# Gate and up projections in a seven-product block form on pairs of segments, and the down projection in groups of two tiles

## The chip, the cores and the metric

One core of a Trainium2 chip runs the whole program in one launch. The metric is the device time of one execution in microseconds (us). A core has five engines that work side by side, each with its own queue, served in order: TensorE (PE, matrix products; its weight loads are shown as PEld), VectorE (DVE), ScalarE (ACT), GpSimd (POOL) and SyncE (SP, here the issuer of DMAs). SBUF is the on-chip memory, PSUM the memory that PE writes its products to, in banks of 128 x 512 fp32 values.

## The reference

```python
h = _layernorm(x) * (1 + ca) + sa
x = x + ga * _A_ref(h, ...)            # attention with a memory, 32 heads, 4 segments of 512 rows
h = _layernorm(x) * (1 + cb) + sb
g = jnp.einsum("bsd,df->bsf", h, w_gate)
u = jnp.einsum("bsd,df->bsf", h, w_up)
x = x + gb * jnp.einsum("bsf,fd->bsd", g * u, w_down)
```

The input is 2048 rows of 512 features, in fp32. sa, ca, ga, sb, cb and gb are six vectors made from a condition vector. The change is in the last three lines, the gated feed-forward part: w_gate and w_up are 512 x 1376, w_down is 1376 x 512.

## The kernel before

The first 522 us of the program hold the modulation vectors, the first LayerNorm, the attention and its output projection (`wo_row`, `wo_add`: the sum of attention and input, 128 rows at a time, goes to a DRAM buffer `x1d` by a DMA on L496). The last stage, from 522 us on, is the feed-forward part, and the change is there. It works on four segments of 512 rows one after the other.

Every fp32 product is made of three products of a faster type, fp32r: each operand is split into a high part (a rounded copy) and a low part (the operand less the high part), and high x high, low x high and high x low are summed in PSUM. The transposed activations of a segment are `chH` and `chL` (512 features as 4 blocks of 128, by 512 rows). 1376 features make 11 tiles (`ft`, `NF`): ten of 128 and the last of 96.

`gate_up(i)` (L1110) makes 12 matmuls for the gate and 12 for the up projection of tile i (4 blocks x 3 products, L1122), each into a bank of its own. ACT copies the gate bank to SBUF (`gs`, L1126), DVE multiplies it by the up bank (L1127), ACT makes the high part `mH` (L1130) and DVE the low part `mL` (L1131). The down projection of tile i (L1143) then takes 12 matmuls: 4 row blocks x 3 products, into four banks `acc` that stay open over all 11 tiles of the segment. `gate_up(i + 1)` is issued before the down products of tile i, so that PE has work while the other engines make `mH` and `mL`. At a segment's end DVE adds the four banks to the rows of `x1d`, loaded again (`xc`, L1155 and L1156), and the result is stored (L1157).

Weights are prepared once and then stay in SBUF. `prep(i)` (L394) loads tile i of w_gate, w_up and w_down (L400, L402), makes the high parts on DVE (L429) and the low parts on POOL (L430); w_down is first multiplied by gb (`gbb`, DVE, L435), then split on ACT (L437) and POOL (L438). Tiles 0 and 1 are prepared before the last stage, on POOL alone; tiles 2 to 10 during segment 0. `lnC(s)` (L504) is the second LayerNorm of a segment. It loads four row blocks of `x1d` and calls `ln` (L171): statistics on DVE (L178), a few small operations, the normalisation on DVE (L198), 16 transposes on PE (L88), scale and shift on ACT (`chf`, L211), then the high and low parts (for segment 0 on ACT and POOL, L218 and L219; else on DVE, L215 and L216). For segments 1 to 3 it runs inside the segment before, at tiles 3 and 6.

PSUM has eight banks. They are named by tags: `ms0`, `ms1`, `tb`, `sm`, `lq0`, `lq1`, and `lk`, which is one tile of two banks. The order in which each engine issues its instructions is set by a scheduler when the program is built; `pe()` and `pin()` (L72, L79) add an ordering after the PE instruction issued before, without a wait.

Of the kernel before, what the change touches and what calls it, by code (L numbers as in the profile page):

```python
# [17 lines left out]
P = 128  # L18
# [39 lines left out]
def tile_kernel(ctx, tc, x, wq, wk_, wv, wo, beta, w_gate, w_up, w_down, c, w_mod, out):  # L58
# [28 lines left out]
    def TP(*a):  # L87
        return pe(nc.tensor.transpose(*a))  # L88
# [4 lines left out]
    wpool = ctx.enter_context(tc.tile_pool(name="wp", bufs=1))  # L93
# [298 lines left out]
    wt = {}  # L392

    def prep(i, pool, rpool, tag, nb):  # L394

        f0, n = ft[i]
        r, raws = {}, {}
        for w, nm in ((w_gate, "g"), (w_up, "u")):
            raws[nm] = raw = rpool.tile([P, KT, P], F32, tag=tag, name=f"cr{nm}{i}", bufs=nb)
            pin(nc.sync.dma_start(raw[:, :, 0:n], w.rearrange("(k p) f -> p k f", p=P)[:, :, f0:f0 + n]))  # L400
        rawd = rpool.tile([P, D], F32, tag=tag, name=f"crd{i}", bufs=nb)
        pin(nc.sync.dma_start(rawd[0:n], w_down[f0:f0 + n, :]))  # L402
        yield 0.0
        if i < 2:
            gp = nc.gpsimd
            for nm in "gu":
                hi = pool.tile([P, KT, P], F32R, name=f"{nm}H{i}", bufs=1)
                r[nm] = (hi, pool.tile([P, KT, P], F32R, name=f"{nm}L{i}", bufs=1))
                pin(gp.tensor_copy(hi, raws[nm]))
                yield 0.0  # L410
            for nm in "gu":
                pin(gp.tensor_sub(r[nm][1], raws[nm], r[nm][0].bitcast(F32)))
                yield 0.0
            hi = pool.tile([P, D], F32R, name=f"dH{i}", bufs=1)
            lo = pool.tile([P, D], F32R, name=f"dL{i}", bufs=1)
            pin(gp.tensor_mul(rawd, rawd, gbb))
            yield 0.0
            pin(gp.tensor_copy(hi, rawd))
            yield 0.0
            pin(gp.tensor_sub(lo, rawd, hi.bitcast(F32)))  # L420
            r["d"] = (hi, lo)
            wt[i] = r
            yield 0.0
            return
        for nm in "gu":
            raw = raws[nm]
            hi = pool.tile([P, KT, P], F32R, name=f"{nm}H{i}", bufs=1)
            lo = pool.tile([P, KT, P], F32R, name=f"{nm}L{i}", bufs=1)
            pin(vec.tensor_copy(hi[:, :, 0:n], raw[:, :, 0:n]))  # L429
            nc.gpsimd.tensor_sub(lo[:, :, 0:n], raw[:, :, 0:n], hi[:, :, 0:n].bitcast(F32))  # L430
            r[nm] = (hi, lo)
            yield 0.0
        hi = pool.tile([P, D], F32R, name=f"dH{i}", bufs=1)
        lo = pool.tile([P, D], F32R, name=f"dL{i}", bufs=1)
        pin(vec.tensor_mul(rawd[0:n], rawd[0:n], gbb[0:n]))  # L435
        yield 0.0
        act.activation(hi[0:n], rawd[0:n], AF.Copy)  # L437
        nc.gpsimd.tensor_sub(lo[0:n], rawd[0:n], hi[0:n].bitcast(F32))  # L438
        r["d"] = (hi, lo)
        wt[i] = r  # L440
        yield 0.0

    def wo_load(s, pool):
        rw = []
# [59 lines left out]
    def lnC(s, pool, hpool, xpool, tag, nb):  # L504
        xt = []
        for t in range(4):
            a = xpool.tile([P, D], F32, tag=tag, name=f"x1_{s}_{t}", bufs=nb)
            nc.sync.dma_start(a, x1d[s][t])
            xt.append(a)
        yield 0.1  # L510
        return (yield from ln(pool, hpool, xt, s, cb_c, sb_c, "c", ("h{}", 1, 1), s > 0))


    pwpool, pw = open_pool(name="pw", bufs=1, reuse_waits="tile")
# [426 lines left out]
    def fill_b():  # L941
        open_b()
        pb, bc = B["pb"], B["bc"]
        while osegs[0] <= 2:
            yield None
        us2 = []
        op2 = wo_op(2, B["o", 2], us2)
        xr1 = xr_load(1, pb)
        lg = lnC(0, pb, bc, pb, "x1", 4)
        pr = prep(0, bc, pb, "cr", 3)  # L950
        mm = weave(wo_mm(1, B["us1"], xr1), lg, (3, 6, 8, 10, 12, 14))
        yield from weave(weave(mm, op2, (0, 5, 9, 13)), pr, (6, 11, 11, 13, 14, 15, 16, 18))
        yield from op2
        xr2 = xr_load(2, pb)
        B["orl_free"] = True
        yield from pr
        pr = prep(1, bc, pb, "cr", 3)
        next(pr)
        yield from weave(weave(wo_mm(2, us2, xr2), lg, (0, 2, 4, 6, 8, 10, 12, 14)), pr, (0, 2, 3, 7, 9, 16, 18))
        yield from pr  # L960
        B["nxt"] = yield from lg

    vfree, osegs = [1], [0]
    fa, fb = fill_a(), fill_b()
# [128 lines left out]
    close(B["pbpool"])  # L1093
    close(pwpool)
    close(apool)
    vec.eng = nc.vector


    pcpool, pc = open_pool(name="pc", bufs=2, reuse_waits="tile")
    PC = 12  # L1100
    btag[:] = ["ms", "tb", "ms", "sm"]
    bc = B["bc"]
    nxt = B["nxt"]
    for s in range(NSEG):
        hH, hL = nxt
        ac = psp.tile([P, 2, 512], F32, tag="lk", name=f"acc{s}", bufs=1)
        acc = [pst((P, 512), f"lq{t}", f"acc{s}{t}") for t in range(2)] + [ac[:, t] for t in range(2)]
        mids = {}

        def gate_up(i):  # L1110
            f0, n = ft[i]
            if s == 0 and 1 < i + 1 < NF:
                last_pe[0] = None
                run(prep(i + 1, pc, pc, "pt", PC))
            pss = []
            for nm in "gu":
                ps = bank(f"{nm}ps{s}_{i}")
                hi, lo = wt[i][nm]
                j = 0
                for k in range(KT):  # L1120
                    for a, b in ((hi, hH), (lo, hH), (hi, hL)):
                        nc.tensor.matmul(ps[0:n], a[:, k, 0:n], b[k], start=j == 0, stop=j == 11)  # L1122
                        j += 1
                pss.append(ps)
            gs = pc.tile([P, L], F32, tag="tsb", name=f"gs{s}_{i}", bufs=2)
            act.activation(gs[0:n], pss[0][0:n], AF.Copy)  # L1126
            vec.tensor_mul(gs[0:n], gs[0:n], pss[1][0:n])  # L1127
            mH = pc.tile([P, L], F32R, tag="pt", name=f"mH{s}_{i}", bufs=PC)
            mL = pc.tile([P, L], F32R, tag="pt", name=f"mL{s}_{i}", bufs=PC)
            act.activation(mH[0:n], gs[0:n], AF.Copy)  # L1130
            vec.tensor_sub(mL[0:n], gs[0:n], mH[0:n].bitcast(F32))  # L1131
            mids[i] = mH, mL

        gate_up(0)
        for i in range(NF):
            if i + 1 < NF:
                gate_up(i + 1)
            n = ft[i][1]
            mH, mL = mids.pop(i)
            dH, dL = wt[i]["d"]  # L1140
            for t in range(4):
                for j, (a, b) in enumerate(((mH, dH), (mL, dH), (mH, dL))):
                    nc.tensor.matmul(acc[t], a[0:n, t * P:(t + 1) * P], b[0:n, :],  # L1143
                                     start=i == 0 and j == 0, stop=i == NF - 1 and j == 2)
            if i == 3 and s + 1 < NSEG:
                last_pe[0] = None
                lg = lnC(s + 1, pc, pc if s % 2 == 0 else bc, pc, "pt", PC)
                for _ in range(10):
                    next(lg)
            if i == 6 and s + 1 < NSEG:  # L1150
                last_pe[0] = None
                nxt = run(lg)
        for t in range(4):
            xr = pc.tile([P, D], F32, tag="pt", name=f"xc{s}_{t}", bufs=PC)
            nc.sync.dma_start(xr, x1d[s][t])  # L1155
            vec.tensor_add(xr, xr, acc[t])  # L1156
            nc.sync.dma_start(out[rows(s, t), :], xr)  # L1157
    close(pcpool)
    close(B["bcpool"])

# [25 lines left out]
```

## Time and profile before

| | |
|---|---|
| three runs | 898.5, 898.92, 900.3 us; median 898.92 |
| the profiled execution, first to last instruction (span) | 898.4 us |
| last stage, first matmul to end of the last | 522.0 to 893.9 us |
| loads of a weight tile, issue to landing (median) | 2.9 to 3.6 us |

The busy time of an engine is given in us and as a share of the span, with the number of instructions. A row of a group gives line, engine and operation, the tiles written and read, their shapes, the count, busy time and mean duration in ns, then the idle time of the engine just before and what ended it. The chain that ended last is followed back from the last instruction, at each step to what released it. A row of windows gives the start and end of a stretch, its length, then the busy time of PE, PEld, DVE, ACT and POOL in it, with counts, then the granted clock of PE as a share of full speed, the busy share of the DMA engines, and GB/s. A row of the timeline gives start, duration and the instruction, with the wait before it and its releaser in brackets.

### The profile page before, as it was taken

Reading aid. Unit: us, or ns where it says so; the run is one execution under the profiler, and the core shown is the slowest. Engines: PE = TensorE matmul, PEld = TensorE weight load, DVE = VectorE, ACT = ScalarE, POOL = GpSimd, SP = SyncE. Lnnn points to the kernel's source line nnn. Section 1 sums busy time; section 2 is a strip of 40 time slices with the busy share of each in tenths; the row PEclk is TensorE's granted clock in tenths of the full one; section 3 lists DMA queues with packets and bytes.
Section 4 is the critical chain, followed back from the end, with each engine's and each line's share of the span. In section 5 each row is a group of like instructions: output and inputs, shape, how many; then the busy total and the mean of one; then the engine's idle time right before and its main releaser. Section 6 shows DMA issues by size and latency. Waiting matters only on the chain.

```text
span 898.4 us, 14218 instructions
## 1 busy us (share of the span) xinstructions
PE 870.9 (97%) x5084; PEld 620.5 (69%) x5084; DVE 523.4 (58%) x1579; ACT 406.1 (45%) x601; POOL 321.2 (36%) x470
## 2 busy tenths in 40 slices
PE   8989999989999999999999999999999999999997
PEld 5755656556665556666666678887888788878886
DVE  7698777888788877778887244552133213321112
ACT  3747757687676865777454512231112111211111
POOL 4445536466455763756337516630000000000000
PEclk8999999999999999999999999999999999999999
DMA  7654434454545555365584344321001100110011
GB/s 219 163 159 130 122 109 124 152 154 130 146 111 156 141 154 129 107 202 166 187 243 140 109 144 126 106 73 71 24 1 47 72 24 1 47 45 3 1 47 47
DMA packets 74951, 97.23 MB, mean 108 GB/s; under 512 B 10528, under 2 KB 47392, under 8 KB 74880
## 3 DMA queue, kind: packets, MB, share of 16 engines
q1 hardware_dynamic: 74736, 96.31, 36.3%
q8 instruction: 40, 0.66, 0.3%
q14 instruction: 31, 0.25, 0.1%
q10 hardware_dynamic: 144, 0.02, 0.0%
HBM read 67.98 MB, written 28.05 MB: 107 GB/s over the span
## 4 chain that ended last, share of the span: by engine, by line
PE 81%; DVE 10%; ACT 5%; issue 1%; DMA 1%; POOL 1%; SPq 0%; DVEq 0%; POOLq 0%
PE gps L1122 14%; PE acc L1143 14%; PE ups L1122 14%; PE tb L85 8%; PE q L85 6%; PE k L85 6%; DVE q L39 5%; PE wops L85 5%; PE vps L85 4%; PE kps L85 4%; PE qps L85 2%; ACT pt L331 2%; PE up L85 1%; PE mz L85 1%; PE tr L88 1%
## 5 line engine op out<-in xcount | busy, mean ns | idle before, releaser
L39 DVE CUSTOM_DVE_ANT_0 q<-q,cmask 128x384 f32<-128x384 f32 (+3 forms) x512 | 246.6, 508 | 49.3 <-PE q L85 39.2
L331 ACT ACTIVATE pt<-k 128x1024 f32<-128x1024 f32 x160 | 163.8, 1024 | 64.4 <-PE k L85 63.3
L337 POOL TENSOR_SCALAR_AFFINE_SELECT pt<-pt 128x256 f32<-128x256 f32 (+1 forms) x224 | 96.7, 446 | 166.0 <-ACT pt L331 163.6
L1127 DVE TENSOR_TENSOR gs<-gs,ups 128x512 f32<-128x512 f32 (+1 forms) x44 | 30.2, 687 | 194.9 <-PE ups L1122 194.9
L85 PE MATMUL q<-kst,qst 96*128 96x384 bf16 (+3 forms) x512 | 101.6, 299 | 11.0 <-DVE nm L39 9.7
L85 PE MATMUL k<-qst,kst 98*128 98x384 bf16 (+3 forms) x512 | 97.1, 302 | 5.0 <-ACT pt L331 4.9
L1126 ACT ACTIVATE gs<-gps 128x512 f32<-128x512 f32 (+1 forms) x44 | 26.2, 597 | 146.3 <-PE gps L1122 146.3
L1130 ACT ACTIVATE mH<-gs 128x512 fp32r<-128x512 f32 (+1 forms) x44 | 27.8, 632 | 130.4 <-DVE gs L1127 128.1
L85 PE MATMUL tb<-pt,v 128*32 128x512 f32 (+3 forms) x1024 | 75.5, 436 | 0.0
L39 DVE DVE_READ_ACCUMULATOR2_ANT nm<- 128x1 f32 x512 | 72.2, 141 | 0.0
L85 PEld LDWEIGHTS <-kst 98*128 98x128 bf16 x512 | 37.7, 98 | 49.5 <-issue 43.2
L1122 PE MATMUL gps<-chH,gL 128*128 128x512 f32 (+1 forms) x176 | 69.3, 394 | 0.0
L1122 PE MATMUL gps<-chH,gH 128*128 128x512 f32 (+1 forms) x176 | 69.3, 394 | 0.0
L1143 PE MATMUL acc<-dH,mL 128*128 128x512 f32 (+1 forms) x176 | 69.3, 394 | 0.0
L1122 PE MATMUL ups<-chH,uH 128*128 128x512 f32 (+1 forms) x176 | 69.3, 394 | 0.0
L1122 PE MATMUL gps<-chL,gH 128*128 128x512 f32 (+1 forms) x176 | 69.3, 393 | 0.0
L1143 PE MATMUL acc<-dL,mH 128*128 128x512 f32 (+1 forms) x176 | 69.2, 393 | 0.0
L1122 PE MATMUL ups<-chL,uH 128*128 128x512 f32 (+1 forms) x176 | 69.2, 393 | 0.0
L1122 PE MATMUL ups<-chH,uL 128*128 128x512 f32 (+1 forms) x176 | 69.2, 393 | 0.0
L85 PEld LDWEIGHTS <-qst 96*128 96x128 bf16 x512 | 43.1, 97 | 37.5 <-issue 13.4
L1143 PE MATMUL acc<-dH,mH 128*128 128x512 f32 (+1 forms) x176 | 65.0, 395 | 0.0
L85 PEld LDWEIGHTS tb<-pt,v 128*32 128x32 f32 x1024 | 28.7, 109 | 38.6 <-issue 33.8
(218 smaller groups left out, 1654.5 us busy)
## 6 DMA issues: line engine op xcount, KB each, us to landing
wm<-in_w_mod_dram SPq DMA_DIRECT2D x24, 256.0 KB, 4.0
kd<-k SPq DMA_DIRECT2D x16, 384.0 KB, 2.5
kst<-kd SPq DMA_DIRECT2D x32, 192.0 KB, 3.2
qd<-q SPq DMA_DIRECT2D x16, 384.0 KB, 2.9
qst<-qd SPq DMA_DIRECT2D x32, 192.0 KB, 3.6
x<-in_x_dram SPq DMA_DIRECT2D x16, 256.0 KB, 4.5
kst<-kd SPq DMA_DIRECT2D x32, 128.0 KB, 3.1
qst<-qd SPq DMA_DIRECT2D x32, 128.0 KB, 3.6
```

The lines of the kernel that those rows point to most:

```text
L39: i = getattr(self.eng, name)(*a, **k)
L85: return pe(nc.tensor.matmul(*a, **k))
L88: return pe(nc.tensor.transpose(*a))
L331: ex = act.activation(pt, kp, AF.Exp, scale=0.25)
L337: sels[u, i] = nc.gpsimd.affine_select(w, w, pattern=[[0, w.shape[1]], [1, P]], compare_op=ALU.is_ge, fill=0.0, base=0, channel_multiplier=-1)
L1122: nc.tensor.matmul(ps[0:n], a[:, k, 0:n], b[k], start=j == 0, stop=j == 11)
L1126: act.activation(gs[0:n], pss[0][0:n], AF.Copy)
L1127: vec.tensor_mul(gs[0:n], gs[0:n], pss[1][0:n])
L1130: act.activation(mH[0:n], gs[0:n], AF.Copy)
L1143: nc.tensor.matmul(acc[t], a[0:n, t * P:(t + 1) * P], b[0:n, :], start=i == 0 and j == 0, stop=i == NF - 1 and j == 2)
```

## The change

Gate and up are no longer made segment by segment. The segments form two pairs, p = 0 (segments 0 and 1) and p = 1 (2 and 3). Two tiles of one weight matrix by 512 features are seen as 2 x 2 blocks (two tiles, two halves of the features), and the transposed activations of a pair of segments as 2 x 2 blocks (two halves of the features, two segments). The product of these blocks takes seven products of blocks instead of eight, with sums of blocks on both sides. A `unit` is the gate or up projection of two tiles for a pair of segments: seven products of 6 matmuls (2 blocks of 128 features x 3 products). Its products are called by number: Z (2), Y (5, then 3), X (1, 6, 7, 4). ACT copies of open banks and DVE sums of them give the four blocks of the result.

- `build(p)` makes the seven right-hand pieces of a pair from the fp32 activations `hfs`: eight differences on POOL, high parts on ACT, low parts on DVE. For p = 0, pieces 1 and 2 come from `lnC(0)`.
- `wprep(n)` prepares the seven left-hand pieces of a unit: one load of 512 KB, four additions or subtractions of 256 elements per partition on POOL, then high parts on ACT and low parts on POOL of 512, 256 and 1024 elements. Three slots (`wh0` to `wh2`, `wl0` to `wl2`) hold them; unit n uses slot -n mod 3. `prepare(n + 2)` is issued along unit n.
- Units 0 to 7 are tiles (2,3), (4,5), (6,7), (8,9) of pair 0, gate and up in turn. Unit 8 (`x_unit`) is tile 10 of pair 1 in plain products (`direct`, 48 matmuls), prepared by `xprep`. Units 9 to 18 are tiles (0,1) to (8,9) of pair 1.
- Pair 0 begins with tiles 0, 1 and 10 in plain products: `direct` for segment 0, 24 matmuls each, then the transposes of segment 1's LayerNorm, down chunks of segment 0, then `direct` for segment 1. The second half of `direct` uses product 1 of the first half (`q0_*`) and pieces 5 and 3.
- The product of gate and up is made on POOL where both lie in SBUF (three of four blocks of a pair of units) and on DVE for the one still in PSUM. `split` makes `mH` on ACT and `mL` on DVE.
- `down` takes two tiles at a time (one for tile 10): a chunk of 6 matmuls for a row block goes to one of four banks in turn (`lq0`, first half of `lk`, `lq1`, second half of `lk`), and DVE adds it to an accumulator in SBUF (`xa`), which was loaded from `x1d`. After tiles (8,9) the row block is stored, and for p = 0 the accumulator is loaded for p = 1. `d()` issues one chunk from a list, at the points of a unit given in `DS`.
- `wdprep` loads and splits w_down tile by tile for each pair, so twice: product and low part on DVE, high part on ACT. The down weights of tiles 0, 1 and 10 of pair 0 lie in slot `wh1`/`wl1`.
- `lnC` keeps fp32 activations; segment 1's small operations go to DVE. It runs in the start for segment 1 and in units 1 to 6 for segments 2 and 3.

The diff, cut to its core:

```diff
+    units = [(0, nm, i) for i in range(2, LAST, 2) for nm in "gu"]
+    CH = len(units)
+    units += [(1, "x", LAST)] + [(1, nm, i) for i in range(0, LAST, 2) for nm in "gu"]
...
+    def wprep(n, tag, pool, rpool):
...
+        pin(nc.sync.dma_start(raw.rearrange("p k r c -> p k (r c)"), views["gu".index(nm)][:, :, 0:2 * P]))
...
+        gp.tensor_add(S[:, 0], A(1, 0), A(1, 1))
+        gp.tensor_sub(S[:, 1], S[:, 0], A(0, 0))
+        gp.tensor_sub(S[:, 2], A(0, 0), A(1, 0))
+        gp.tensor_sub(S[:, 3], A(0, 1), S[:, 1])
+        top = raw[:, :, 0].rearrange("p (c k) f -> p c k f", c=2)
+        for d, v in ((slice(4, 6), top), (6, A(1, 1)), (slice(0, 4), S)):
+            act.activation(wh[:, d], v, AF.Copy)
+            gp.tensor_sub(wl[:, d], v, wh[:, d].bitcast(F32))
...
+    def six(ps, wh, wl, wi, n, bh, bl, first, last):
+        c = 0
+        for k in range(2):
+            w, l = (a[(slice(None), *wi(k), slice(0, n))] for a in (wh, wl))
+            for a, b in ((w, bh), (l, bh), (w, bl)):
+                pe(nc.tensor.matmul(ps[0:n], a, b[:, k], start=first and c == 0, stop=last and c == 5, skip_group_check=True))
+                c += 1
...
+    def down(p, fs, c, t):
+        ps = dbank(f"acc{p}_{fs[0]}_{c}_{t}")
...
+        xa = x1a[p, c, t]
+        vec.tensor_add(xa, xa, ps)
...
+    def unit(n):
...
+        Z = pst((P, 512), "sm", f"Z{u}")
+        mm(Z, 2, True, True)
+        yield 1
+        prev(0)
+        Y = pst((P, 512), "tb", f"Y{u}")
+        mm(Y, 5, True, True)
+        p5 = out_of(f"p5{u}", Y)
+        yield 2
+        X = xbank(f"X{u}")
+        mm(X, 1, True, True)
+        finish(p, nm, i, 0, add(f"c0{u}", Z, out_of(f"p1{u}", X)), False)
+        yield 3
+        prev(1)
+        tail.clear()
+        yield 4
+        mm(Y, 3, False, True)
+        yy = out_of(f"y{u}", Y)
+        yield 5
+        mm(X, 6, False, True)
+        finish(p, nm, i, 1, add(f"c1{u}", X, yy), False)
+        yield 6
+        def seven():
+            mm(X, 7, False, True)
+            finish(p, nm, i + 1, 1, add(f"c2{u}", X, p5), False)
+        def four():
+            mm(X, 4, False, True)
+            finish(p, nm, i + 1, 0, X, True)
+            if nm == "u":
+                dq.extend(lambda c=c, t=t: down(p, (i, i + 1), c, t) for c in (1, 0) for t in range(4))
+        tail.extend((seven, four))
...
+    dh = pc.tile([P, 7, 2, P], F32R, tag="wh1", name="dHp", bufs=1).rearrange("p a b c -> p (a b c)")
+    dl = pc.tile([P, 7, 2, P], F32R, tag="wl1", name="dLp", bufs=1).rearrange("p a b c -> p (a b c)")
...
+    DS = {"g": (1, 5, 6), "u": (1, 2, 4, 5, 6), "x": (1, 2, 4)}
```

More of the change, by code (lines that the diff above doesn't have):

```diff
@@ L398, in prep @@
+    def prep(i, pool, rpool):
+        raws = {}
         for w, nm in ((w_gate, "g"), (w_up, "u")):
[L399 to L402, printed above, removed]
+            raws[nm] = raw = rpool.tile([P, KT, P], F32, tag="cr", name=f"cr{nm}{i}", bufs=4)
+            pin(nc.sync.dma_start(raw, w.rearrange("(k p) f -> p k f", p=P)[:, :, i * P:(i + 1) * P]))
@@ L403, in prep @@
         yield 0.0
[L404 to L416, printed above, removed]
+        gp = nc.gpsimd
@@ L1095, in tile_kernel @@
     close(apool)
+    close(wppool)
     vec.eng = nc.vector
     pcpool, pc = open_pool(name="pc", bufs=2, reuse_waits="tile")
-    PC = 12
-    btag[:] = ["ms", "tb", "ms", "sm"]
     bc = B["bc"]
[L1103 to L1157, printed above, removed]
@@ new lines, in tile_kernel, with lns @@
+    lgs = []
+    def lns():
+        for s in (2, 3):
+            yield from lnC(s, pc, (bc, pc)[s % 2], pc, "t", NT, dbank)
+    lg = lns()
+    for n in range(NU):
+        p, nm, i = units[n]
+        pr = prepare(n + 2)
+        if n == CH - 1:
+            nb = build(1)
+        for st in (unit if nm != "x" else x_unit)(n):
+            next(pr, None)
+            if n == 0:
+                next(pr1, None)
+                next(nb, None)
+            if st in DS[nm] and n < NU - 1:
+                d()
+            if 1 <= n < CH - 1:
+                next(lg, None)
+            if n == CH - 1 and st in (1, 3, 5, 6) or n == CH:
+                next(nb, None)
+        run(pr)
+        if n == CH - 2:
+            run(lg)
```

360 lines of the change are left out of this document (323 added, 37 removed).

## The prediction

> **What bounds the kernel now.** I read the page first (busy times, clock, chain that ended last), then the windows of the last stage, then its chain in order of time, its groups by shape, and the timeline of DVE, POOL and SP at its start.
>
> ```profile
> span 898.4 us, 14218 instructions
> PE 870.9 (97%) x5084; PEld 620.5 (69%) x5084; DVE 523.4 (58%) x1579; ACT 406.1 (45%) x601; POOL 321.2 (36%) x470
> PE 81%; DVE 10%; ACT 5%; issue 1%; DMA 1%; POOL 1%; SPq 0%; DVEq 0%; POOLq 0%
> ...
> 500.00:522.00 22.00, 20.32 (x120) 14.91 (x121) 5.77 (x10) 6.75 (x11) 7.53 (x7) 1.00 0.24 86
> 534.00:574.00 40.00, 40.00 (x174) 32.32 (x173) 23.99 (x39) 9.93 (x18) 24.84 (x22) 1.00 0.39 112
> 574.00:894.00 320.00, 319.89 (x1409) 257.92 (x1407) 89.36 (x148) 57.78 (x94) 16.55 (x21) 1.00 0.11 36
> ...
> 646.42 2.79 PE gps L1122 x12
> 649.21 2.80 PE ups L1122 x12
> 652.01 2.73 PE acc L1143 x12
> ...
> 679.51 1.75 PE ctp L88 x16
> ...
> 888.31 5.59 PE acc L1143 x24
> 893.90 0.02 issue
> 893.92 0.69 DVE xc L1156
> ...
> L1122 PE MATMUL gps<-chH,gH x176: 387/394/404, 522.0 to 884.7; 128*128 128x512 f32 x160, 128*96 128x512 f32 x16
> L1143 PE MATMUL acc<-dL,mH x176: 388/393/404, 533.9 to 893.5; 128*128 128x512 f32 x160, 96*128 96x512 f32 x16
> ```
>
> Window rows give length, then busy time of PE, PEld, DVE, ACT and POOL, the granted clock, DMA share and GB/s. The stage that changes runs from 522.0 to 893.9 us. PE is busy in all of it (40.00 of 40, 319.89 of 320), at clock 1.00, and the chain is matmul after matmul. So here a matmul left out is worth its whole slot, and any wait put before one costs its whole length: nothing else is left to hide it. The spare engines: from 574 on POOL works 16.55 us of 320, DVE 89.36, ACT 57.78.
>
> **The change, part by part.**
>
> *Matmuls.* Six of the nine groups of 176 stand on L1122, three on L1143: 1584 matmuls, plus 48 transposes. Sixteen transposes take 1.75 us, 48 take 5.2, so one matmul has (893.9 - 522.0 - 5.2) / 1584 = 0.231 us. Gate and up need 24 matmuls for each of 11 tiles and 4 segments, 1056, now. After: a unit (gate or up of two tiles on two segments) takes 7 x 6 = 42 instead of 48. There are 8 units in the first pair and 10 in the second, 756; the plain tiles take 144 at the start (tiles 0, 1, 10 of the first pair) and 48 in the second (tile 10): 948. Down stays at 528, transposes at 48. So 108 go, **-25.0 us**; without any wait the span would be 898.4 - 25.0 = 873.4.
>
> *What is added beside PE.* Weights are now prepared for every unit, not once: POOL does four additions of 256 elements and three low parts of 512, 256 and 1024, 2816 in all, and three of four gate-up products (512 each) come to it per pair of units.
>
> ```profile
> L1131 DVE TENSOR_TENSOR mL<-gs,mH 128x512 fp32r<-128x512 f32 x40 | 28.9, 723 | 25.7 <-ACT mH L1130 25.6
> L1127 DVE TENSOR_TENSOR gs<-gs,ups 128x512 f32<-128x512 f32 x40 | 27.5, 687 | 168.7 <-PE ups L1122 168.7
> L1130 ACT ACTIVATE mH<-gs 128x512 fp32r<-128x512 f32 x40 | 25.3, 632 | 118.9 <-DVE gs L1127 116.6 <-issue 2.3
> L1156 DVE TENSOR_TENSOR xc<-xc,acc 128x512 f32<-128x512 f32 x16 | 10.3, 684 | 18.3 <-PE acc L1143 17.9 <-issue 0.4
> L178 DVE BATCH_NORM_STATS2 cst<-x 128x6 f32<-128x512 f32 x12 | 7.6, 679 | 0.0
> L198 DVE TENSOR_SCALAR x<-x,cmv,cy 128x512 f32<-128x512 f32 x12 | 5.7, 540 | 0.4 <-POOL cy L195 0.4
> L435 DVE TENSOR_TENSOR crd<-crd,gbb 128x512 f32<-128x512 f32 x8 | 11.6, 1447 | 0.4 <-DMA crd<-in_w_down_dram 0.4
> ...
> 547.15 1.78 DVE L435 TENSOR_TENSOR crd<-crd,gbb 128x512 f32<-128x512 f32 x1
> ...
> 547.03 1.35 POOL L430 TENSOR_TENSOR gL<-crg,gH 128x512 fp32r<-128x512 f32 x1 [2.93 <-DVE gH L429]
> 548.35 1.74 POOL L430 TENSOR_TENSOR uL<-cru,uH 128x512 fp32r<-128x512 f32 x1
> 550.05 1.28 POOL L438 TENSOR_TENSOR dL<-crd,dH 128x512 fp32r<-128x512 f32 x1
> ...
> x<-x1d SPq DMA_DIRECT2D x4, 256.0 KB, 3.5
> ```
>
> A 512-element POOL subtraction takes 1.28 us alone (550.05). I size other POOL operations by elements, 2.5 ns each (0.64 and 2.56 us), with half as much and twice as much as bounds. A pair of units then needs (2 x 2816 + 3 x 512) x 2.5 ns = 17.9 us of POOL, beside 2 x 42 + 48 = 132 matmuls, 30.5 us. DVE reads PSUM in 15 operations (additions, product, eight down sums) of 0.69, 10.3 us, and does 8 from SBUF alone (four splits, four for w_down); ACT has about 12 us. All fit under 30.5 if they overlap freely. They don't quite: the DVE product that begins at 547.15 needs about 0.55 alone, but ends at 548.93, 0.58 after POOL's operation (547.03 + 1.35); the next POOL operation takes 1.74 instead of 1.28. SBUF-only work of DVE with two inputs and POOL take turns. POOL and those eight together are 17.9 + 8 x 0.6 = 22.7 of 30.5 us; that leaves the steady state covered, but not places where more comes together.
>
> *Loads.* Gate, up and down weights are read twice: 33 more loads of 256 KB, 8.7 MB in 372 us, 23 GB/s beside 36 in a row with DMA at 0.11. They start two units (some 20 us) ahead against 3.5 us to land. SP's queue gets them with no wait that PE sees: 0, at most one landing (3.5).
>
> The new waits, in order (value; bounds):
>
> 1. *Start: 9.5 us (0 to 16).* Before, segment 1's LayerNorm came in the middle of segment 0; now both are needed in the first 27 us. PE can fill only 72 matmuls of segment 0, 16 transposes and 36 down matmuls, 26.6 us, to 548.6. Then the first matmul of piece 5 (difference of the segments) must find its data. Lower bound: loads after the last x1d store (523.3), 3.5 landing, four times 0.68 and 0.54, then transposes, ACT, POOL difference and split, some 6 more: 538, no wait. Upper: DVE's other work there stands in the same queue (6 products and splits, 6 w_down, 8 sums, small ones), about 24 us with LayerNorm and builds, and alternates with 14 us of POOL (first unit's weights, tile 10, differences): 527 + 38 = 565, 16 late. Walking both queues in issue order gives 558; I take that, as the turns above were strict. Behind it: down's third bank shares a tile with the fourth, so a chunk waits for a DVE sum behind splits that wait for POOL.
> 2. *Units 0 and 1: 4 (1 to 6).* Each product Z, Y, X reuses a bank that an ACT copy or DVE sum must free; those stand behind splits (0.63 and 0.72) and build pieces still in the queue.
> 3. *Unit 2's weights: 5 (2.4 to 6.5).* Their slot holds the down weights of tiles 0, 1, 10 until the last matmul of unit 1. Only then ACT (0.63) and POOL (1.28) make what Z's second matmul needs: 2.4 with handovers. Product Y needs the third low part, 0.64 + 2.56 later; 11 matmuls cover 2.5 of it. So 2.4 + 0.8 at least where DVE stays out, and up to 6.5 with DVE's turns.
> 4. *LayerNorm 2 and 3 inside units 1 to 6: 1.5 (0 to 4)*: 24 DVE operations of 0.54 to 0.68 ahead of sums.
> 5. *Turn to the second pair: 5.5 (0 to 8).* Fourteen more ACT/DVE splits, eight differences and tile 10 come into units 7 to 10: a DVE sum or split that comes late by one or two POOL operations (1.28 to 2.56) each time holds a bank or a down chunk; four such places make 5.5, none 0.
> 6. *Second pair and last unit: 2.5 (0 to 5).* The last unit has no down chunks between its products, so a sum (0.69) stands open about once; at the end five left-over chunks (1.4 us each) cover the last splits.
>
> Sum 28 (3 to 46): 873.4 + 28.0 = 901.4 against the span of 898.4. The median of the runs (898.92) stands 0.5 above that span, so the floor without waits is 873.9 in the median, and the forecast **902 us**.
>
> *The clock.*
> ```profile
> 10.00:20.00 10.00, 8.75 (x56) 7.46 (x57) 9.11 (x23) 3.10 (x5) 2.40 (x5) 0.74 0.80 253
> 20.00:30.00 10.00, 10.00 (x37) 8.21 (x36) 7.20 (x13) 7.60 (x13) 0.00 (x0) 0.74 0.18 54
> 22.26 0.63 PE L85 MATMUL kps<-ahH,wkH 128*128 128x512 f32 x1
> 22.68 0.63 PE L85 MATMUL kps<-ahH,wkL 128*128 128x512 f32 x1
> ```
> Between 10 and 30 us PE had gaps, the clock was 0.74, and matmuls came 0.42 us apart instead of 0.23; between 500 and 522 waits of 1.7 us in all left it at 1.00. Some of the new waits are longer than those. I take 0 in the sum and make the other end a rival. [...]
>
> **The rivals.**
>
> *The first waits pay for the later ones: 888 us, faster.* While PE stands at the start, POOL and DVE work on, and weights and pieces for later units run ahead. Then of the six waits only the first and second stay (13.5): 873.9 + 13.5 = 887.4, and small rests make 888. For it: the 30.5 against 22.7 us above, and POOL's 16.55 of 320 us. Against: unit 2's slot cannot run ahead, and queues are first in, first out. It decides if waits 3 to 6 come to less than 9.7 us (23.2 in all, 897.1).
>
> *DVE and POOL become the bound to unit 10: 911.* Up to there POOL and SBUF-only DVE have, at the durations above, about 60 us in PE's 68 (start to unit 1), 64 in 78 (units 2 to 6) and 60 in 64 (7 to 10): 184 in 210. If each of some 98 such DVE operations makes a POOL operation 0.45 longer (1.74 against 1.28), 44 are added: 228, 18 over, beside the start's 14 and 5 later: 873.9 + 37. For it: the alternation; against: operations that read PSUM kept 0.69.
>
> [...]
>
> *The change does not remove what it says: 899.* If the scheduler's order made PE run its old count or wait exactly as long. The count is fixed in the program, so this has little weight.
>
> **How the numbers follow.** A measurement of this kernel can tell 0.2% (1.8 us): same is 897.1 to 900.7. Forecast as above, 892 to 912: 0.50, of which 0.13 lies under 897.1, 0.11 within, 0.26 above. First waits pay: 0.28, faster. Bound by DVE and POOL: 0.12, slower. Clock: 0.07, slower. Nothing removed: 0.03, same. Faster 0.41, same 0.14, slower 0.45. The forecast's own range is 892 to 912; for 8 in 10 it has to reach to the first rival (881) and past the second (914).
>
> **What would show it.** Right: PE's count falls by 108, from 5084 to about 4976; after 522 us PE has gaps, the largest before piece 5 (about 549) and at unit 2's first and second products, put down to ACT or POOL making the weights; waits on DVE's sums at units 0 and 1 and around units 7 to 9; POOL after 534 at 150 us or more instead of 41 (24.84 + 16.55); w_down's DVE products above 0.6 us on average. Wrong: gaps under 15 us in sum (the first rival), DVE or POOL over 90% busy from 550 to 730 (the second), clock under 1.00 after 522 (the third), or waits for a DMA, which I put at nothing.

## The result, and the profile after

The changed kernel takes **905.54 us** (median of four runs, 904.63 to 906.35) against 899.61 for the kernel before: ratio 1.0069, 95% interval 1.0054 to 1.0084. It is slower by 5.9 us. Forecast were 902, a range of 881 to 914, and slower with a chance of 0.45. The profiled execution has a span of 903.1 us and took 904.86.

From the page of the changed kernel: span, busy times, and the chain by engine.

```profile
span 903.1 us, 14396 instructions
PE 856.8 (95%) x4975; PEld 600.8 (67%) x4976; DVE 655.1 (73%) x1711; ACT 475.5 (53%) x725; POOL 501.2 (56%) x607
PE 71%; DVE 11%; ACT 6%; POOL 6%; DMA 3%; issue 2%; SPq 0%; DVEq 0%; POOLq 0%; ACTq 0%
```

PE has 109 matmul records fewer (108 are gone by count, a record can be missing) and 14.1 us less busy time, not 25. In the last stage the chain passes through DVE, ACT, POOL and DMAs, where it was PE alone up to the last matmul. DVE has 132 us more, POOL 180.

Windows of the changed kernel (columns as before: length, PE, PEld, DVE, ACT, POOL, granted clock, DMA share, GB/s):

```profile
522.00:534.00 12.00, 11.45 (x50) 8.75 (x48) 7.11 (x14) 5.53 (x11) 1.42 (x1) 1.00 1.05 337
...
549.00:560.00 11.00, 7.97 (x29) 5.69 (x28) 7.74 (x9) 2.08 (x4) 8.49 (x7) 0.84 0.27 95
...
604.00:612.00 8.00, 5.25 (x15) 3.62 (x15) 5.53 (x7) 3.34 (x6) 7.99 (x7) 0.79 0.30 87
...
709.00:724.00 15.00, 10.24 (x36) 7.03 (x37) 12.93 (x14) 6.27 (x12) 15.00 (x11) 0.89 0.05 19
...
780.00:860.00 80.00, 80.00 (x347) 64.61 (x346) 43.62 (x61) 29.11 (x50) 49.10 (x40) 1.00 0.12 34
```

Between 780 and 860 us the seven-product form runs as meant: PE busy in all 80.00 us, POOL 49.10 and DVE 43.62. The loss is in three places where the clock is below 1.00 as well. PE's long waits there, from its timeline (start, duration, instruction, in brackets the wait before it and what ended it):

```profile
553.15 0.65 PE L1271 MATMUL acc<-dHp,mH 128*128 128x512 f32 x1 [2.95 <-DVE xa L1274]
...
575.87 0.40 PE L1216 MATMUL Yu<-bL,uH 128*128 128x512 f32 x1
578.39 0.50 PE L1216 MATMUL Zg<-bh,cwH 128*128 128x512 f32 x1 [2.13 <-DVE c1u L1304]
578.72 0.39 PE L1216 MATMUL Zg<-bh,cwL 128*128 128x512 f32 x1
...
604.58 0.50 PE L1216 MATMUL Zg<-bh,cwH 128*128 128x512 f32 x1 [0.48 <-ACT cwH L456]
607.35 0.50 PE L1216 MATMUL Zg<-bh,cwL 128*128 128x512 f32 x1 [2.27 <-POOL cwL L457]
711.23 0.50 PE L1216 MATMUL Xu<-bH,cwH 128*128 128x512 f32 x1 [2.25 <-DVE c2u L1304]
717.07 0.72 PE L1271 MATMUL acc<-dH,mH 128*128 128x512 f32 x1 [2.12 <-ACT mH L1240]
...
772.32 0.50 PE L1216 MATMUL Xg<-bH,cwH 128*128 128x512 f32 x1 [1.29 <-DVE c1g L1304]
```

All 17 waits after 521 us add to 19.15 us; the seven above are the start's fourth down chunk, unit 0, unit 2's weights (two rows), the turn to the second pair (two rows), and one in the second pair.

The last stage's end, from the chain:

```profile
876.76 22.69 PE acc L1271 x96
899.45 0.02 issue
899.47 0.69 DVE xa L1274
```

Without waits the last matmul would end at 893.9 - 25.0 = 868.9. It ends at 899.45: **the 25.0 us saved are given back, and 5.5 more: 30.5 in all.** Waits are 19.15 of them.

What the waits cost beyond their length is seen after the first one:

```profile
552.00:554.00 2.00, 0.85 (x2) 0.68 (x3) 1.70 (x3) 0.00 (x0) 2.00 (x2) 0.84 1.00 359
554.00:556.00 2.00, 2.00 (x6) 1.58 (x5) 0.03 (x1) 0.00 (x0) 1.92 (x3) 0.50 0.12 39
556.00:558.00 2.00, 2.00 (x8) 1.51 (x8) 1.56 (x3) 0.00 (x0) 1.56 (x2) 0.81 0.00 0
...
553.60 0.63 PE L1271 MATMUL acc<-dHp,mL 128*128 128x512 f32 x1
554.02 0.63 PE L1271 MATMUL acc<-dLp,mH 128*128 128x512 f32 x1
```

At clock 0.50 matmuls come 0.42 us apart. With full clock outside, the three rows give (0.16 x 2 + 0.50 x 2 + 0.19 x 2) / 0.50 = 3.4 us at half clock. The windows at 604 and 709 give the same: 0.21 x 8 / 0.5 and 0.11 x 15 / 0.5, 3.4 and 3.3. Three such stretches lose at most 1.7 us each, 5 us in all; counted by the matmuls in them, some 20 at 0.42 to 0.43 us instead of 0.23, it is about 4.

Why DVE was late: its timeline in the start of the changed kernel, and POOL's beside it.

```profile
567.54 4.41 DVE L1179 TENSOR_TENSOR bL<-t,bH 128x512 fp32r<-128x512 f32 x1 [1.76 <-ACT bH L1178]
571.87 0.68 DVE L1304 TENSOR_TENSOR c1g<-Yg,q 128x512 f32<-128x512 f32 x1
572.48 0.68 DVE L1179 TENSOR_TENSOR bL<-t,bH 128x512 fp32r<-128x512 f32 x1
```
```profile
567.06 1.29 POOL L1299 TENSOR_TENSOR c1g<-c1g,c1u 96x512 f32<-96x512 f32 x1
568.31 0.74 POOL L457 TENSOR_TENSOR cwL<-cr,cwH 128x256 fp32r<-128x256 f32 x1
569.01 2.39 POOL L457 TENSOR_TENSOR cwL<-cs,cwH 128x1024 fp32r<-128x1024 f32 x1
```

A split of 0.68 us (572.48) took 4.41 at 567.54, and ended 0.55 after three POOL operations in a row (569.01 + 2.39 = 571.40). Behind it in the queue stood the sums that free the banks for unit 0. From 521 us on, the 24 splits of that line took 0.68 to 4.41 us; the 95 sums of L1274, which read PSUM, took 0.67 to 0.69, with a POOL operation beside them (57) or without. In the kernel before, the nine w_down products of L435, with two inputs from SBUF, took 0.68 to 1.78, and the casts of L429, with one input, at most 0.42, beside POOL too. These are not strict turns, though: the split let three POOL operations pass, where the product at 547.15 in the kernel before stood behind one. What decides which of the two goes first, no run shows. The sum at 571.87, which reads PSUM, kept 0.68.

### The profile page after: what moved, and what is told of

It reads as the page before. It is cut to its first block, busy times and chain, and to the rows that moved or that the text cites. A ratio compares the mean times of both kernels' runs of the same rounds, so it can differ in the third digit from the quotient of the medians.

```text
span 903.1 us, 14396 instructions
## 1 busy us (share of the span) xinstructions
PE 856.8 (95%) x4975; PEld 600.8 (67%) x4976; DVE 655.1 (73%) x1711; ACT 475.5 (53%) x725; POOL 501.2 (56%) x607
## 4 chain that ended last, share of the span: by engine, by line
PE 71%; DVE 11%; ACT 6%; POOL 6%; DMA 3%; issue 2%; SPq 0%; DVEq 0%; POOLq 0%; ACTq 0%
PE acc L1271 12%; PE tb L85 8%; PE q L85 6%; PE k L85 6%; PE Xg L1216 5%; PE Xu L1216 5%; DVE q L39 5%; PE wops L85 5%; PE vps L85 4%; PE kps L85 4%; PE Yg L1216 3%; PE Yu L1216 3%; PE qps L85 2%; POOL cwL L457 2%; ACT pt L331 2%
## 5 line engine op out<-in xcount | busy, mean ns | idle before, releaser
L331 ACT ACTIVATE pt<-k 128x1024 f32<-128x1024 f32 x160 | 163.8, 1024 | 64.5 <-PE k L85 63.4
L1274 DVE TENSOR_TENSOR xa<-xa,acc 128x512 f32<-128x512 f32 x95 | 64.7, 682 | 48.0 <-PE acc L1271 46.6
L1271 PE MATMUL acc<-dL,mH 128*128 128x512 f32 (+1 forms) x150 | 59.3, 396 | 0.0
L457 POOL TENSOR_TENSOR cwL<-cr,cwH 128x512 fp32r<-128x512 f32 (+1 forms) x36 | 40.1, 1131 | 21.5 <-ACT cwH L456 21.4
L457 POOL TENSOR_TENSOR cwL<-cs,cwH 128x1024 fp32r<-128x1024 f32 x18 | 48.3, 2684 | 1.2 <-ACT cwH L456 1.2
L1299 POOL TENSOR_TENSOR c0g<-c0g,c0u 128x512 f32<-128x512 f32 x9 | 11.7, 1296 | 56.4 <-DVE c0u L1304 37.7
L363 ACT ACTIVATE tsb<-tb 128x512 f32<-128x512 f32 x32 | 19.0, 595 | 41.0 <-PE tb L85 41.0
L1271 PEld LDWEIGHTS acc<-dH,mH 128*128 128x128 f32 (+1 forms) x150 | 28.2, 188 | 9.9 <-ACT mH L1240 2.5
L1271 PEld LDWEIGHTS acc<-dH,mL 128*128 128x128 f32 (+1 forms) x150 | 28.3, 189 | 7.3 <-DVE mL L1241 0.9
L1271 PEld LDWEIGHTS acc<-dL,mH 128*128 128x128 f32 (+1 forms) x150 | 28.3, 188 | 6.7
L1216 PE MATMUL Xu<-bH,cwH 128*128 128x512 f32 (+1 forms) x68 | 28.1, 413 | 3.5 <-DVE c2u L1304 2.7
```

Source lines behind the costliest of these rows:

```text
L331: ex = act.activation(pt, kp, AF.Exp, scale=0.25)
L363: act.activation(tsbs[u], tbs.pop(u), AF.Copy)
L457: gp.tensor_sub(wl[:, d], v, wh[:, d].bitcast(F32))
L1216: pe(nc.tensor.matmul(ps[0:n], a, b[:, k], start=first and c == 0, stop=last and c == 5, skip_group_check=True))
L1271: pe(nc.tensor.matmul(ps, a[0:m, t * P:(t + 1) * P], b[0:m], start=j == 0, stop=j == n - 1))
L1274: vec.tensor_add(xa, xa, ps)
```

## The experiments

The theory at the outset: the saved matmuls are worth their full slot, and the loss lies in a few separate waits and in the half-clock stretches behind them. The rival: POOL and DVE carry one backlog through the stage, so that a wait taken away in one place comes back in another, or the saved matmuls were hidden anyway. Differences below are between ratios to the kernel before, on the same chip, times 899.6; the changed kernel has 1.0069. Two of these ratios can be told apart if they differ by more than about 0.002 (1.8 us). Single profiles are compared by their waits and not by their spans: the stage's first matmul stands anywhere from 519.8 to 522.5 us in them.

**Is the saving real?** One line in `unit`:

```diff
+        mm(Z, 2, True, True)
         mm(Z, 2, True, True)
```

> The changed kernel with product 2 of each of the 18 units issued twice (the second overwrites the first, so the result is unchanged): 18 x 6 = 108 matmuls more, as many as the change takes out. Theory (a matmul is worth 0.231 us in nearly all of this stage, and the loss lies in a few waits): 25 us more, less 2 to 6 us by which POOL and DVE catch up ahead of unit 2 and the turn, so 925 to 929. Rival (POOL and DVE set the pace of the units, the matmuls that were taken out stood beside them): 905 to 912.

Measured: 930.51 us, ratio 1.0346 (1.0330 to 1.0362), **24.9 us more** (about 2 either way) for 108 matmuls: 0.231 us each, the full price. The waits did not shrink (20.96 us in sum against 19.15), though POOL and DVE had 25 us more in the stage. So the first half of the theory stands, the rival that the matmuls were hidden falls, and so does my 2 to 6 us of catching up. One thing did change: the wait at the fourth down chunk was as long as in the changed kernel, and the clock stayed up behind it.

```profile
552.69 0.50 PE L1271 MATMUL acc<-dHp,mH 128*128 128x512 f32 x1 [2.96 <-DVE xa L1274]
...
549.00:560.00 11.00, 7.89 (x35) 5.34 (x34) 7.67 (x9) 1.61 (x3) 8.06 (x7) 1.00 0.31 95
```

**Does the lower clock cost time of its own?**

```diff
+        if t == 3:
+            dummy(pst((P, 512), "tb", "dum"), wds[0, 0][0][:, 0:P], wds[0, 0][0], 11)
         down(0, (0, 1), 0, t)
...
+        if n == 2:
+            dummy(Z, wslot[1][0][:, 4, 0], pieces[0, 1][0][:, 0], 12)
         mm(Z, 2, True, True)
...
+        if (p, fs[0], c, t) == (0, LAST - 2, 1, 0):
+            dummy(ps, wds[0, LAST - 2][0][:, 0:P], wds[0, LAST - 2][0], 8)
```

> The changed kernel with 31 matmuls more, whose results nobody reads: 11 ahead of the fourth down chunk at the start, 12 ahead of unit 2's first product, 8 ahead of the first chunk after unit 7, each in a wait that the trace of the changed kernel shows (2.95, 2.75 and 2.12 us). Theory (the three stretches of 3.4 us at half clock follow from these waits and cost time of their own): no half-clock stretch after 522 us, and 4 to 5 us less, about 901. Rival (the waits alone decide, PE at half pace only fills time in which it would wait later): 905 to 906, the same as the changed kernel. Second rival (matmuls added are time added): 31 x 0.231 = 7.2 us more, 912 to 913.

Measured: 903.21 us, ratio 1.0045 (1.0033 to 1.0057), 2.2 us less with 31 matmuls more; a little outside of what can be told from nothing. In its windows the clock stays up behind the filled waits, but falls at a wait of 2.13 us that had done no harm in the changed kernel:

```profile
549.00:560.00 11.00, 10.36 (x45) 7.41 (x44) 8.00 (x9) 2.64 (x5) 9.12 (x8) 1.00 0.31 97
574.00:582.00 8.00, 5.87 (x19) 4.38 (x18) 7.86 (x8) 3.65 (x6) 8.00 (x6) 0.79 0.10 29
```

The same window of the changed kernel, with the same 5.87 us of PE:

```profile
574.00:582.00 8.00, 5.87 (x26) 4.44 (x25) 7.85 (x8) 3.29 (x6) 8.00 (x6) 1.00 0.05 15
```

So what a wait of this length does to the clock is not settled by its length. There is one stretch at half clock instead of three, and about half of the expected 4 to 5 us was saved; that fits. It is weak evidence: the profiled executions differ by 0.2 us only (902.9 against 903.1, the stage beginning at the same time in both). That the lower clock costs time rests more on the matmuls 0.42 us apart than on this run.

**Are the waits separate?** Four runs say no, one says yes. The yes:

```diff
-        i = nd[0] % 4
+        i = nd[0] % 3
...
+        if i < 2:
+            return pst((P, 512), f"lq{i}", name)
+        lkt[0] = psp.tile([P, 2, 512], F32, tag="lk", name=name, bufs=1)
+        return lkt[0][:, 0]
```

> Down chunks go round three banks instead of four, so that no chunk waits for the sum of another half of the same two-bank tile. Theory (the 2.95 us before the fourth chunk at the start come from that shared tile): that wait falls to under 1 us, and with it the first half-clock stretch (1.6): 3 to 4 us less, about 902. Rival (DVE's queue is the limit at the start, the sums come late by themselves): the wait moves to the next chunks or to the first product with piece 5, and the time stays at 904 to 906.

Measured: 901.94 us, ratio 1.0026 (1.0013 to 1.0038), 3.9 us less, as expected. The wait of 2.95 and the two small ones before it (0.40, 0.34) are gone, 1.93 remains at the next chunk, and the clock stays at full there. The rest of the stage has waits in the same places. But the clock's part of the forecast did not come as told: the turn has two half-clock stretches in this profile (0.23 x 15 / 0.5 = 6.9 us) where the changed kernel has one, so three in all as before.

```profile
709.00:724.00 15.00, 11.56 (x37) 7.96 (x36) 11.93 (x12) 6.96 (x12) 15.00 (x11) 0.77 0.21 71
```

The waits add to 17.12 us, 2.0 less; the number fits better than its reasons.

Unit 2's slot set free earlier:

```diff
-            if st in DS[nm] and n < NU - 1:
+            if (st in DS[nm] or n < 2) and n < NU - 1:
```

> One condition changed: units 0 and 1 issue a down chunk at each of their six steps, so that the chunks that read the down weights of tiles 0 and 1 are done by unit 1's second step, and unit 2's weights can be written to that slot some 6 us earlier. Theory (unit 2's 2.75 us and the half-clock stretch behind it come from this slot): 2.7 + 1.4 = about 4 us less, 901 to 902, with no PE wait over 1 us at unit 2. Rival (POOL is the limit there, about 6 us of weights and products in its queue before): the wait stays over 2 us and the time at 904 to 906.

Measured: 912.97 us, ratio 1.0148 (1.0131 to 1.0165), **7.1 us more**. PE no longer waits for unit 2's weights. But the chunks had been cover, and where they are missing other waits lie open; from its timeline:

```profile
587.24 0.50 PE L1271 MATMUL acc<-dHp,mH 96*128 96x512 f32 x1 [1.98 <-DVE xa L1274]
619.00 0.79 PE L1271 MATMUL acc<-dH,mH 128*128 128x512 f32 x1 [2.77 <-ACT mH L1240]
620.11 0.80 PE L1271 MATMUL acc<-dH,mL 128*128 128x512 f32 x1 [0.32 <-DVE mL L1241]
624.79 1.85 PE L88 MATMUL ctp<-ident,x 128*128 128x128 f32 x4 [2.16 <-DVE x L557]
```

7.2 us of new waits stand against 2.75 removed, and the clock is 0.92 between 582 and 604 and 0.94 between 612 and 700, where it was 1.00.

The build steps at the turn, moved later:

```diff
-            if n == CH - 1 and st in (1, 3, 5, 6) or n == CH:
+            if n == CH - 1 and st in (1, 3, 5, 6) or n == CH and st > 2:
```

> Only the place of three build steps of the second pair is changed: the differences t2, t3, t4 and their splits are issued in the second half of unit 8, not in the first. Theory (at the turn POOL, 15.00 us busy of 15, makes the product c2g late behind two of these differences, and DVE the sum c2u behind their splits): the waits of 2.25, 2.12 and 0.40 us and the half-clock stretch go, 5 to 6 us less, about 900. Rival (POOL has the same work in any order, so the wait moves to unit 9, which needs t2 and t4): under 2 us less, 904 to 906.

Measured: 905.82 us, ratio 1.0073 (1.0056 to 1.0091): no difference. The waits for mH and mL are gone, 2.25 became 1.60, and some 50 us later this stands:

```profile
764.84 0.50 PE L1216 MATMUL Xu<-bH,cwH 128*128 128x512 f32 x1 [3.50 <-DVE c2u L1304]
```

Two down chunks kept for the turn:

```diff
-            if st in DS[nm] and n < NU - 1:
+            if st in ((1, 4, 6) if n == CH - 1 else DS[nm]) and n < NU - 1:
```

> The changed kernel, with two of the five down chunks of unit 7 kept back, so that unit 8 can issue them at the turn. Theory (at the turn PE waits because sums and a product come late from DVE and POOL, and work of its own that is ready covers that): each chunk is 1.4 us; the waits of 2.25 and 2.12 us fall to about 1 in sum and the half-clock stretch behind them goes: 4 us less, 901 to 902. Rival (as with the early chunks: the wait moves to where the chunk is taken away): 904 to 907.

Measured: 904.79 us, ratio 1.0060 (1.0045 to 1.0076): 0.8 us less, not to be told from nothing. The 4.77 us at the turn became 3.19, and a wait of 4.07 for c2u came at 764.45, as in the run before this one.

Four mends together:

```diff
-        i = nd[0] % 4
+        i = nd[0] % 3
...
-            gp.tensor_sub(wl[:, d], v, wh[:, d].bitcast(F32))
+            (vec if n in (1, 2) else gp).tensor_sub(wl[:, d], v, wh[:, d].bitcast(F32))
...
+    d(2)
     for n in range(NU):
...
-            if st in DS[nm] and n < NU - 1:
+            if st in ((1, 4, 6) if n == CH - 1 else DS[nm]) and n < NU - 1:
```

> Four edits together on the changed kernel: three banks for the down chunks, the low parts of units 1 and 2 on DVE (unit 2's wait), two chunks ahead of unit 0's first product (its wait of 2.13 us), two chunks of unit 7 kept for unit 8. Theory (separate waits at separate places, so the savings add): 3.6 for the banks (measured), 2 to 3.5 at unit 2, 1 to 1.5 at unit 0, 4 at the turn: 893 to 896, faster than the kernel before. Rival (DVE and POOL hand the same backlog on from place to place): 900 to 904.

Measured: 901.73 us, ratio 1.0026 (1.0012 to 1.0041): what the banks give alone, and nothing from the other three. Unit 0's and unit 2's waits are gone, and in their place stand these, with the one at the turn:

```profile
603.68 0.50 PE L1216 MATMUL Xu<-bH,cwH 128*128 128x512 f32 x1 [3.32 <-DVE c1u L1303]
615.41 0.50 PE L1270 MATMUL acc<-dH,mL 128*128 128x512 f32 x1 [1.94 <-DVE mL L1240]
...
714.69 0.79 PE L1270 MATMUL acc<-dH,mL 128*128 128x512 f32 x1 [2.74 <-DVE mL L1240]
```

The theory of separate waits falls here: three of the four savings did not add. That most waits are places where one backlog shows fits all four runs.

**Whose backlog?** Work moved from POOL to DVE, in `finish` and in `wprep`:

```diff
-        (vec if psum else nc.gpsimd).tensor_mul(g[0:n], g[0:n], v[0:n])
+        vec.tensor_mul(g[0:n], g[0:n], v[0:n])
```

> The product of gate and up is always made on DVE, never on POOL: 31 operations of about 1.3 us go from POOL, 31 of about 0.7 us come to DVE. Theory (POOL and the SBUF-only work of DVE take turns at one resource, and DVE needs it half as long): the wait for mH at the turn (2.12 us, behind c2g on POOL) and the half-clock stretch behind it go or shrink, 2 to 5 us less, 900 to 903. Rival (the two engines overlap, and DVE's queue is the one that is full): sums come later, more waits for DVE, 906 to 912.

Measured: 909.93 us, ratio 1.0115 (1.0100 to 1.0129), 4.1 us more. The wait for mH at the turn went, as expected, but the sum c2u before it is later:

```profile
718.02 0.79 PE L1216 MATMUL Xu<-bH,cwH 128*128 128x512 f32 x1 [5.00 <-DVE c2u L1304]
...
714.48 1.21 DVE L1179 TENSOR_TENSOR bL<-t,bH 128x512 fp32r<-128x512 f32 x1
715.62 0.67 DVE L1274 TENSOR_TENSOR xa<-xa,acc 128x512 f32<-128x512 f32 x1
716.21 1.15 DVE L1252 TENSOR_TENSOR dL<-crd,dH 96x512 fp32r<-96x512 f32 x1
717.29 0.68 DVE L1304 TENSOR_TENSOR c2u<-Xu,p5u 128x512 f32<-128x512 f32 x1
```

Here DVE's queue is the one with the late sums.

```diff
-            gp.tensor_sub(wl[:, d], v, wh[:, d].bitcast(F32))
+            vec.tensor_sub(wl[:, d], v, wh[:, d].bitcast(F32))
```

> The low parts of the units' weights (512, 256 and 1024 elements per unit) are made on DVE, not on POOL: 18 x 4.5 us go from POOL, 18 x 2.4 come to DVE. Theory (taking turns, as in the run with the products): unit 2's wait falls from 2.75 to about 1.5 us and the turn's waits shrink, but a DVE operation of 1.3 us now stands ahead of sums: 2 us less to 2 us more, 903 to 907. Rival (DVE's queue is the full one): several waits for DVE sums in every unit, 910 to 925.

Measured: 904.48 us, ratio 1.0059 (1.0047 to 1.0071): 0.9 us less, not to be told from nothing, and inside what the theory gave. Unit 2's wait fell from 2.27 to 0.40, unit 0's from 2.13 to 1.29; at the turn a wait of 2.48 for mL on DVE came. DVE is busy for 271 us of the stage here and POOL for 144, against 249 and 227 in the changed kernel. So the relief of POOL and the load on DVE about cancel here. The rival of this run (910 to 925) falls, while the run before it bore its rival out (906 to 912).

Banks and products together, the two edits above:

```diff
-        i = nd[0] % 4
+        i = nd[0] % 3
...
-        (vec if psum else nc.gpsimd).tensor_mul(g[0:n], g[0:n], v[0:n])
+        vec.tensor_mul(g[0:n], g[0:n], v[0:n])
```

> Three banks for the down chunks and all products of gate and up on DVE, together. Theory: the two savings add, since one lies at the start and the other at the turn: 3.6 (measured for the banks alone) and 2 to 5, so 897 to 900. Rival (what is gained at the start is waited for at the turn): no more than the better of the two, 902.

Measured: 906.89 us, ratio 1.0088 (1.0070 to 1.0106). Neither expectation: the products alone cost time, and the sum of the two measured differences (-3.9 and +4.1) is +0.2, measured +1.7.

Last, work taken away instead of moved.

```diff
-            gp.tensor_sub(wl[:, d], v, wh[:, d].bitcast(F32))
+            act.activation(wl[:, d], v, AF.Copy)
```

> The changed kernel with the low parts of the units' weights made by ACT as copies of the values; the subtraction is left out, so the output isn't the reference's. 18 x 4.5 us go from POOL, 18 x about 2.1 come to ACT, DVE keeps its queue. Theory (POOL's work makes the backlog, by its own queue and by keeping DVE's SBUF-only work out): the waits of unit 0 (2.13), unit 2 (2.75) and the turn (4.77 and 1.69 behind it) and the half-clock stretches go, 10 to 15 us less, 890 to 895. Rival (DVE's queue is the limit by itself): the waits for DVE's sums stay, only unit 2's wait goes: 900 to 903.

Measured: 897.45 us, ratio 0.9979 (0.9971 to 0.9988), 8.1 us less than the changed kernel. POOL has 138.75 us in the stage instead of some 227; the splits `bL` of differences fall from a mean of 1479 ns to 1062. That is between the theory and its rival. Up to 3 of the 8.1 us are the clock: the profile has one half-clock stretch instead of three. Set beside the run with these low parts on DVE, POOL has about the same work (139 and 144 us), DVE 226 instead of 271, and the time is 7 us less: once POOL is relieved, DVE's share counts.

```diff
-                vec.tensor_sub(lo[:, k], srcs[k], hi[:, k].bitcast(F32))
+                act.activation(lo[:, k], srcs[k], AF.Copy)
...
-        vec.tensor_sub(lo[0:n], r[0:n], hi[0:n].bitcast(F32))
+        act.activation(lo[0:n], r[0:n], AF.Copy)
```

> The changed kernel with the low parts of the right-hand pieces and of w_down made by ACT as copies; the subtraction is left out there, so the output isn't the reference's. About 44 SBUF-only operations (some 48 us with their waits) go from DVE, POOL keeps its work and loses what kept it waiting. Theory (DVE's queue is the one where sums stand behind work that waits for POOL): the waits for DVE at the start (2.95), unit 0 (2.13) and the turn go, unit 2's stays: 10 to 14 us less, 891 to 896. Rival (POOL is the limit): the waits for DVE shrink little, 900 to 904.

Measured: 893.96 us, ratio 0.9933 (0.9917 to 0.9948), **12.2 us less**. Whole-stage windows of the changed kernel, of the run with POOL relieved, and of this one:

```profile
522.00:899.50 377.50, 358.15 (x1525) 280.52 (x1523) 248.54 (x325) 139.15 (x239) 227.45 (x185) 0.99 0.24 74
```
```profile
522.00:892.00 370.00, 354.81 (x1519) 277.86 (x1518) 226.03 (x322) 169.57 (x293) 138.75 (x131) 1.00 0.24 74
```
```profile
522.00:890.00 368.00, 355.36 (x1516) 280.54 (x1514) 197.89 (x277) 161.02 (x285) 212.51 (x185) 0.98 0.24 74
```

89 us off POOL gave 8.1 us, 51 us off DVE gave 12.2. DVE's relief took the start's 2.95 away, left 1.04 of unit 0's 2.13, took the c2u wait at the turn, and left unit 2's (2.41) and mH's (2.04). In the changed kernel DVE is busy 66% of this window and POOL 60%; busy shares don't tell which of the two counts. Both runs relieve POOL or DVE and also remove meetings of the two, since a split or a POOL operation less is one less to wait for; how much comes from DVE's queue and how much from these meetings is not shown. What remains in the last run (12.42 us of waits, and a lower clock in three places: 0.89 from 534 to 549, 0.87 from 604 to 612, 0.79 from 709 to 724) was not looked into further, and no run relieved both engines.

## Why the prediction was right, point by point

**The direction.** Slower had 0.45 and faster 0.41, so the forecast of 902 was nearly an even bet on it.

**Matmuls, -25.0.** Right: 108 fewer, and 0.231 us each by the run with product 2 twice.

**The six waits, 28.** Five of six places were right, most sizes too large; the measured waits add to 19.15:

| step | forecast | waits measured |
|---|---|---|
| 1 start | 9.5 | 6.97 (eight waits; first product of tile 10 with piece 5 at 559.34, forecast 558) |
| 2 units 0 and 1 | 4 | 2.13 |
| 3 unit 2's weights | 5 | 2.75 |
| 4 LayerNorm 2 and 3 | 1.5 | 0 |
| 5 turn | 5.5 | 4.77 |
| 6 second pair, last unit | 2.5 | 2.53 (0.40 + 1.29 + 0.84) |

In step 1 the time came true, but not the cause that I gave first. No matmul waited for piece 5: the last split issued before its product ended at 553.70, and the product began at 559.34, right behind a down chunk. What made it late were the waits ahead of it, the longest on the bank of the fourth down chunk, which the prediction had as an afterthought, and a half-clock stretch. Step 4 cost nothing. The POOL sizes held for 512 and 1024 elements (means of 1.30 us for c0g and 2.68 for the largest low parts, against 1.28 and 2.56 taken); low parts of 256 took 0.83 against 0.64. One reading was off: 0.55 us for a DVE product alone, where the same operation takes 0.68 in the kernel before (538.52); the product at 547.15 ends 0.55 behind POOL's operation, not 0.58.

**The clock, 0.** Wrong: three stretches of 3.4 us at half pace, 4 to 5 us that the sum did not have. A lower clock had a chance of 0.07 as a rival by itself, beside the main forecast; in fact it came with the waits of that forecast. No run had shown what such a fall costs behind a wait of this length; here each stretch loses at most 1.7 us (3.4 at clock 0.50). That sum 28 and measured 30.5 agree is luck: waits forecast 9 too long made room for the clock and for some 7 that I had not counted. More than half of these 7 are the waits again. The trace counts a wait from the end of the matmul before, 0.39 us after its start, while matmuls in a row start 0.23 apart; and the second matmul behind a wait starts 0.33 after the first. So the wait of 2.13 at unit 0 cost 0.26 more than its length (starts at 575.87, 578.39 and 578.72), and the 15 waits ahead of such matmuls cost about 4 us more. The other matmuls start 0.2321 us apart on average against 0.2313 before, about 1 us over 1400. Some 2 us stay unaccounted for.

**Span and median, +0.5.** Mis-sized. In each run of the changed kernel that lists both, the time is 1.7 to 1.8 us above the span (904.86 and 903.1). Before, 898.4 + 1.8 = 900.2 would make its profiled execution the slowest of the three (900.3), not one below the median; that is inferred, not listed.

**Loads, 0.** Right for PE's waits; none ended with a DMA. But at the start the DMA share is 1.05 over 12 us, and the first weights of unit 0 landed 6.42 us after issue, not 3.5, which made POOL start on them at 537.75. Part of the start's lateness is this; no run changed the order of these loads, so its share stays open.

**The rivals.** "The first waits pay for the later ones" fell, but not by much: by its own sign, waits 3 to 6 had to come to less than 9.7 us, and they came to 10.05. The run with product 2 twice speaks against it more clearly: with 25 us more of PE work in the stage, PE's waits did not shrink. "DVE and POOL become the bound to unit 10" fell as priced: from 550 to 730 DVE was busy 131.6 us of 180 and POOL 127.3, not over 90%, and PE was full for 88 us on end (612 to 700). Both were full only near PE's waits (7.85 and 8.00 of 8 us from 574 to 582, 9.00 of 9 each from 700 to 709, 12.93 and 15.00 of 15 at the turn). What it rests on, POOL and SBUF-only DVE work standing in each other's way, is there (a split of 0.68 us took 4.41 at 567.54; in the kernel before, a POOL subtraction of 1.28 took 1.74 at 548.35 beside a DVE product); how much of the 19.15 us it makes no run shows.

## What to carry to other kernels

When one engine is busy from end to end and bounds the time, a product left out is worth its full slot (here 0.231 us a matmul), and so is each wait that its bookkeeping brings; count the second as carefully as the first, with the slow start behind each wait (0.33 us to the second matmul, not 0.23), and look at what stands in front of each bank-freeing sum in its queue, not at busy shares. Work moved between two engines that get in each other's way (here a DVE split of 0.68 us took up to 4.41 beside POOL) need not become cheaper: one such move cost 4.1 us and the other gained nothing that could be measured. Waits with one backlog behind them move when one is mended, and filler work taken from a place leaves a hole there.

## What the runs showed of the hardware

After some waits of 2 to 3 us the clock was at half for 3.4 us. In the changed kernel waits of 2.95, of 0.48 + 2.27, and of 2.12 (with 2.25 some 6 us ahead) were each followed by such a stretch, and one of 2.13 was not; in the run with added matmuls that same 2.13 was, and in the run with product 2 twice a wait of 2.96, at the place of the 2.95, was not. Executions of one kernel differ in it, too: the twelve with three banks have mean clocks of 0.987 to 0.993 and times of 899.4 to 903.6 us, and one stretch takes an estimated 0.002 off the mean clock (3.4 x 0.5 of 900 us). The three stretches of the changed kernel come out alike (3.4, 3.4 and 3.3 us), and the turn of the run with three banks had 6.9 us, as much as two. What sets a stretch off, and why the same wait had one behind it in one run and none in another, no run shows.
